# The fifth group's first dense product without a seven-block set, and the order of the pieces around two batches of attention steps

## The chip, the core and the metric

The kernel runs on one core of a Trainium2 chip. Its time is the device time of one execution in microseconds (us); the figure of a kernel is the median of its runs. The profile's own clock, the span, goes from the first to the last instruction and is a little shorter than the time of the same execution.

## The reference

A decayed linear attention with blocks of 64 positions feeds a two-layer network with a tanh GELU. Cut to what is computed:

```python
batch, n_heads, seq, head_dim = (4, 8, 768, 64)       # q, k, v
for b in range(nb):                                    # blocks of 64
    intra = np.einsum('bhic,bhjc->bhij', qb, kb) * Dmask[None]
    intra = np.einsum('bhij,bhjd->bhid', intra, vb)
    inter = np.einsum('bhid,bhde->bhie', qb * lam_pow[None], kv_state)
    out[:, :, sl] = intra + inter
    kb_dec = kb * rev_pow[None]
    kv_state = lam_block[None, :, None, None] * kv_state + np.einsum('bhsd,bhse->bhde', kb_dec, vb)
...
x = np.ascontiguousarray(attn_out.transpose(0, 2, 1, 3)).reshape(B * S, H * D)   # 3072 x 512
h = x @ w_in                                           # 512 x 2048
g = 0.5 * h * (1.0 + np.tanh(c * (h + 0.044715 * h * h * h)))
return (g @ w_out).astype(np.float32)                  # 2048 x 512
```

## The kernel before

The attention runs in 24 steps, each of 256 positions of one sequence and half of the heads. For a step n, `load_step` brings q, k and v from memory (queue SP), `prep_qk` scales q on DVE and casts k on ACT into one half-precision tile and sends that tile through a transposing DMA (queue SP, steps from 9 on) into `qkT_n`, and `prep_v` scales v on GpSimd (POOL) and then issues the loads of step n + 3. `scores` multiplies (PE, tiles S), `causal` masks the scores on DVE into `PT_n`, and the state is updated with `update`: a DVE addition into t and a POOL product into u. The output of a step goes through ACT into `xT`, the input of the dense part.

Late steps come in batches. `burst(ns, ss)` issues the scores of the steps ns, the attention output (L424, L449) of the earlier steps ss and the state products (L438, tiles K) of ns, then the masks, then the ACT copies into xT, then the first state update of ns.

The dense part works on seven groups of rows: `groups = [[0, 1], [2], [3], [4, 5], [6, 7], [8, 9], [10, 11]]`, each entry 256 positions of a sequence. The group with number 4, the fifth, covers the steps 12 to 15 and has 512 rows. Its work is cut into pieces, kept in the list `filler`, which `fill(n)` takes from the front, n at a time, wherever the hand-written order of the main part (L904 to L1088) says so. So the order on TensorE is written out: pieces of dense work between the attention's steps.

A plain piece of a 512-row group's first product is `mm1([f])`: four matmuls of 128 x 512 into one PSUM bank (Hps), and one ACT gelu from that bank into `gT`. Sixteen such pieces make the product, in the order f = 0, 8, 1, 9, and so on. The two last groups, 5 and 6, use seven block products in place of eight (`seven(m, k)`): the matrices are halved both ways, sums of input blocks (`sum_x`, DVE) and of weight blocks (`sum_win`, DVE) are formed ahead, and each of seven products m = 1 to 7 is four matmuls of 128 x 256 into the banks HX, HW and HY. Copies (ACT, DVE) and additions (DVE) combine them; the products 1, 6, 7 and 4 follow each other in one bank HX, and what is copied or added out of it between two of them reads that bank. One set k covers four values of f, thus the work of four plain pieces.

Before the change, group 4 (`MIXED`) does one of its four sets, k = 0, in this way: ten pieces, seven of them block products and three plain ones set between, then nine plain pieces. The second product of the group (`product`, tiles MX, MW, MY, also in seven-block form) follows; it needs sums of rows of gT (`sum_g`, DVE, tiles gs), which `behind(k, ...)` hangs behind the k-th piece of the group. The sums of the first half of gT hang behind piece n1 - 7 = 12, counted from 0.

The pools matter here. All PSUM tiles come from eight banks (tag "M"); a new tile waits until the earlier one in its bank was read. `qkT` tiles come from four buffers, PT from three, v16 and qk16 from five, the loaded q32, k32 and v32 from four each. The tiles m1, q and u2 of a seven-block set use buffers of q32 and k32, and the sums xs use one of the three xT buffers.

The main part around the change: group 4 is queued in `R(17, 15)` (L1045). Nine pieces of the group before it are left and are done by the first piece after L1059. Eleven pieces are taken between L1057 and the batch of steps 18 and 19 (L1064), and six between that and the batch of 20 and 21 (L1073).

Of the kernel before, what the change touches and what calls it, by code (L numbers as in the profile page):

```python
# [15 lines left out]
def kernel(  # L16
# [43 lines left out]
    def load_step(s, names="qkv"):  # L60
        b, r = divmod(s, 2 * NSB)
        sb, half = divmod(r, 2)
        ts = ld32.setdefault(s, [])
        for nm, src in (("q", q), ("k", k), ("v", v)):
            if nm not in names:
                continue
            t = ld.tile([P, HH, 2, D], FP32, tag=nm + "32", name=f"{nm}32_{s}")
            rows = src[b, half * HH : (half + 1) * HH, sb * SB : (sb + 1) * SB, :]
            queue = nc.scalar if (nm, s) == ("v", 0) else nc.sync
            pin(queue.dma_start(out=t[:].rearrange("p h j d -> p h (j d)"),  # L70
                                in_=rows.rearrange("h (p j) d -> p h (j d)", j=2)))
            ts.append(t)
# [5 lines left out]
    HF, HE = NF // 2, DM // 2  # L78
# [91 lines left out]
    def load_ahead(s):  # L170
        if s < NSTEP:
            load_step(s)
# [83 lines left out]
    def prep_v(s):  # L256
        scale_v(s)
        if s >= 6:
            if s + 3 == FIRST_DMA_T + 1:
                load_step(s + 3, "qk")  # L260
            else:
                load_ahead(s + 3)

    def scale_v(s):
        tv = a16p.tile([P, 2, HH, D], FP16, tag="v16", name=f"v16_{s}")
        pin(nc.gpsimd.tensor_tensor(wide(tv[:]), ld32[s][2][:], decay(dv, s), ALU.mult))  # L266
        a16[s] = a16[s] + (tv,)

    def prep_qk(s):
        cast_qk(s)  # L270
        transpose_dma(s)

    def cast_qk(s):
        q32, k32, _ = ld32[s]
        tqk = a16p.tile([P, 2, 2, HH, D], FP16, tag="qk16", name=f"qk16_{s}")
        tq, tk = tqk[:, 0], tqk[:, 1]
        q_eng = nc.gpsimd if s == 3 else nc.vector
        pin(q_eng.tensor_tensor(wide(tq), q32[:], decay(dq, s), ALU.mult))  # L278
        if s == 0:
            inverse(halves[0])  # L280
            odd(halves[1])
            inverse(halves[1])
        pin(nc.scalar.activation(out=wide(tk), in_=k32[:], func=AF.Copy))  # L283
        a16[s] = (tq, tk)
        whole_qk[s] = tqk
# [3 lines left out]
    def transpose_dma(s):  # L289
        tqk = whole_qk.pop(s)  # L290
        if s >= FIRST_DMA_T:
            o = qkp.tile([P, 2, 2, 2, P], FP16, tag="qkT", name=f"qkT_{s}")
            pin(nc.sync.dma_start_transpose(out=o[:].rearrange("p a j h t -> p (a j h) t"),
                                            in_=tqk[:].rearrange("p a j h d -> p (a j h d)")))
            qkT[s] = o
            if s == FIRST_DMA_T:
                load_step(s + 1, "v")
# [219 lines left out]
        return gs_kept[1:]  # L517

    SEVEN = (5, 6)
    MIXED = 4  # L520
    sum_xs = []
    SLOTS = {5: {1: 0, 2: 1, 5: 1, 6: 1, 3: 1, 7: 1}, 4: {1: 0, 2: 1, 5: 0, 6: 1, 3: 1, 7: 1}}
    groups = [[0, 1], [2], [3], [4, 5], [6, 7], [8, 9], [10, 11]]
    group_of = {sb: (g, i) for g, sbs in enumerate(groups) for i, sb in enumerate(sbs)}
    filler = []

    def queue_group(g, lead=0, per_set=0):
# [12 lines left out]
        def mm1(fs):  # L540
            Hps = ps_M.tile([P, per, N], FP32, tag="M", name="Hps")
            for i, f in enumerate(fs):
                for c in range(NC):
                    pin(nc.tensor.matmul(by_block(Hps[:, i, :]), w_in16[:, c, f * P : (f + 1) * P],  # L544
                                         x(c), start=(c == 0), stop=(c == NC - 1)))
            f = fs[0]
            dst = gT[:, f, :, :] if per == 2 else gT[:, f % HF, f // HF : f // HF + 1, :]
            pin(nc.scalar.activation(out=dst, in_=Hps[:], func=AF.Gelu_apprx_tanh))  # L548
# [151 lines left out]
        def seven(m, k):  # L700

            st = of_set.setdefault(k, {})
            for name in {1: "X", 2: "W", 5: "Y"}.get(m, ""):
                key = name + str(k % 2) if name == "X" else name
                if key not in hbank:
                    hbank[key] = ps_M.tile([P, 2, SB], FP32, tag="M", name="H" + name)
                st[name] = hbank[key]
            dst = st[{2: "W", 5: "Y", 3: "Y"}.get(m, "X")]
            a, b = X_FACTORS[m]
            for i in range(2):  # L710
                f = 2 * k + i
                for c in range(2):
                    pin(nc.tensor.matmul(  # L713
                        dst[:, i, :],
                        w_in_block(a, slice(c, c + 1), slice(f * P, f * P + P))[:, 0],
                        x_block(b, slice(c, c + 1))[:, 0],
                        start=(m in (1, 2, 5) and c == 0 and i == 0), stop=(m in (2, 3, 4) and c == 1),
                        skip_group_check=True))

            def copied(name, tag, eng):  # L720
                t = ld.tile([P, HH, 2, D], FP32, tag=tag, name=f"{name}_{g}_{k}")
                t = t[:].rearrange("p h j d -> p (h j d)").rearrange("p (i t) -> p i t", i=2)
                if eng is nc.scalar:
                    pin(nc.scalar.activation(out=t, in_=dst[:], func=AF.Copy))
                else:
                    pin(eng.tensor_copy(out=t, in_=dst[:]))
                st[name] = t

            def gelu(F, T, src):
                pin(nc.scalar.activation(out=gT[:, 2 * k : 2 * k + 2, F, T * SB : T * SB + SB],  # L730
                                         in_=src, func=AF.Gelu_apprx_tanh))

            def added(F, T, name):
                pin(nc.vector.tensor_tensor(st[name], dst[:], st[name], ALU.add))
                pending.append(lambda src=st[name]: gelu(F, T, src))

            if m == 1:
                copied("m1", "q32", nc.scalar)
            elif m == 2:
                added(0, 0, "m1")  # L740
            elif m == 5:
                copied("q", "q32", nc.scalar)
                release()
            elif m == 6:
                copied("u2", "k32", nc.vector)
            elif m == 3:
                added(0, 1, "u2")
            elif m == 7:
                added(1, 1, "q")
            elif m == 4:  # L750
                pending.insert(0, lambda: gelu(1, 0, dst[:]))
            if (k == HF // 2 - 1 or g == MIXED) and m in (3, 7, 4):
                release()

        def merge(lead, per_set):
# [71 lines left out]
        def behind(k, i0, i1, ms):  # L827

            piece = filler[at + k]

            def both():
                piece()
                sum_g(i0, i1, ms)

            filler[at + k] = both
# [3 lines left out]
        if g in SEVEN:  # L839
# [6 lines left out]
            for k, m in enumerate((2, 4, 3)):  # L846
                behind(len(parts) * k, 4, 8, (m,))
            return
        if g == MIXED:
            sum_xs.append(sum_x)  # L850
            plain = [[f] for i in range(2, HF) for f in (i, i + HF)]
            for m in (1, 0, 2, 5, 0, 6, 3, 0, 7, 4):
                filler.append((lambda m=m: seven(m, 0)) if m else (lambda fs=plain.pop(0): mm1(fs)))
            for fs in plain:
                filler.append(lambda fs=fs: mm1(fs))
        for i in range(HF) if g != MIXED else ():
            for fs in ([[i, i + HF]] if per == 2 else [[i], [i + HF]]):
                filler.append(lambda fs=fs: mm1(fs))
        for m, p in order:
# [3 lines left out]
        n1 = HF * (2 // per)  # L863
        if per == 2:
            behind(5, 0, 4, (1, 2))
            behind(6, 0, 4, (4, 3))
            behind(7, 4, 8, (1,))
            behind(8, 4, 8, (2,))
            behind(9, 4, 8, (4,))
            behind(10, 4, 8, (3,))  # L870
        else:
            n1 += 3 * (g == MIXED)
            behind(n1 - 7, 0, 4, (1, 2) if g == 3 else (1, 2, 4, 3))
            if g == 3:
                behind(12, 0, 4, (4, 3))
            w = 2 if g + 1 in SEVEN else 1
            for k, m in zip((0, 3, 7, 11) if w == 2 else (0, 1, 2, 4), (1, 2, 4, 3)):
                behind(n1 + k, 4, 8, (m,))

    def fill(n):  # L880
        for _ in range(min(n, len(filler))):
            filler.pop(0)()
# [17 lines left out]
    def U(n):  # L900
        update(n, 1)
# [152 lines left out]
    sum_win(4, 0, nc.vector)  # L1054
    fill(2)
    sum_win(4, 1, nc.vector)
    for m in (1, 2, 3, 4):  # L1057
        sum_xs[0](m)
    prep_qk(20)  # L1059
    fill(3)  # L1060
    prep_qk(21)
    fill(8)

    burst((18, 19), (16, 17))  # L1064
    prep_v(20)
    fill(2)
    U(18)
    U(19)
    prep_v(21)
    fill(2)  # L1070
    prep_qk(22)
    fill(2)
    burst((20, 21), (18, 19), 11, 4)  # L1073
# [43 lines left out]
```

## Time and profile before

| | us |
|---|---|
| runs | 203.12, 202.26, 202.57 |
| median | 202.57 |
| the profiled execution, its time | 203.12 |
| its span | 201.3 |

The chain of work that ended last takes 81% of the span on PE, 6% in DMA, 5% on DVE and 4% in the SP queue. The granted TensorE clock is 0.998. The work that the change touches lies between 113 and 132 us. All of the span before 113 us is issued by lines that the change leaves as they are.

A row of the timeline has the start in us, the duration, the engine, the line and operation, the output and input tiles with their shapes, and in brackets how long the engine had been idle before it and what ended that. A row of the chain has start, duration and the work that stood on the chain there. In a table by stretches each engine has its busy time and number of instructions; the granted clock, the DMA engines' share and GB/s come last. Matmuls are pipelined, so that the duration of one in the timeline is longer than its distance to the next one.

### The profile page before, as it was taken

How to read it: one execution, taken by the hardware profiler on the slowest of the kernel's cores; microseconds unless marked ns; L12 is line 12 of the kernel's file. 1: busy time of each engine (PE TensorE's matmuls, PEld its weight loads, DVE VectorE, ACT ScalarE, POOL GpSimd, SP SyncE). 2: the span in 40 equal slices, each digit the busy share in tenths (PEclk: the TensorE clock that was granted, in tenths of full speed). 3: DMA queues.
4: the chain of work that ended last, by engine and by line, in shares of the span. 5: the costliest groups of instructions: out<-in, count | busy, mean ns of one | idle time of the engine just before them, and what ended most of it. 6: DMA issues, size and time to landing. Idle time of an engine off the chain costs nothing.

```text
span 201.3 us, 5970 instructions
## 1 busy us (share of the span) xinstructions
PE 192.3 (96%) x2451; PEld 141.5 (70%) x2451; DVE 159.8 (79%) x304; ACT 123.8 (61%) x253; POOL 74.7 (37%) x85
## 2 busy tenths in 40 slices
PE   8979999999999999998999989799999999999993
PEld 2546544456888888653689855468888888888882
DVE  4888623689999989969989969999778997588720
ACT  2663878375883774677535676563668845778321
POOL 6594123457458633638334204729002030002000
PEclk9999999999999999999999999999999999999999
DMA  5999999999999999997985944940112200020205
GB/s 165 292 327 385 387 384 382 290 288 314 333 249 214 265 260 212 263 249 144 284 192 129 247 150 85 266 72 0 31 24 104 103 10 0 0 107 0 107 0 208
DMA packets 61722, 37.86 MB, mean 188 GB/s; under 512 B 17536, under 2 KB 54656, under 8 KB 61696
## 3 DMA queue, kind: packets, MB, share of 16 engines
q1 hardware_dynamic: 61152, 37.23, 73.2%
q8 instruction: 19, 0.31, 0.7%
q10 hardware_dynamic: 544, 0.26, 0.5%
q14 instruction: 7, 0.06, 0.1%
HBM read 27.26 MB, written 6.29 MB: 167 GB/s over the span
## 4 chain that ended last, share of the span: by engine, by line
PE 81%; DMA 6%; DVE 5%; SPq 4%; issue 1%; ACT 1%
PE Hps L544 18%; PE MX L621 17%; PE MY L621 9%; PE HX L713 8%; PE O2ps L559 7%; PE MW L621 4%; PE HY L713 4%; SPq L70 4%; DMA wi<-in_moe_w_in_dram 4%; PE Hps L804 3%; PE S L340 3%; DMA qkT<-qk 3%; PE HW L713 2%; DVE gs L591 2%; DVE PT L350 2%; PE OK L398 2%
## 5 line engine op out<-in xcount | busy, mean ns | idle before, releaser
L501 POOL TENSOR_TENSOR u<-t,lumask 128x256 f16<-128x256 f32 x40 | 30.6, 780 | 51.3 <-DVE t L494 28.0
L544 PE MATMUL Hps<-xT,w_in 128*128 128x512 f16 (+1 forms) x272 | 47.7, 329 | 0.5 <-DVE PT L350 0.5
L544 PEld LDWEIGHTS <-w_in 128*128 128x128 f16 x272 | 26.2, 98 | 17.4 <-issue 0.6
L548 ACT ACTIVATE gT<-Hps 128x512 f16<-128x512 f32 x52 | 30.7, 602 | 8.7 <-PE Hps L544 8.2
L621 PEld LDWEIGHTS <-gs 128*128 128x128 f16 x320 | 31.2, 98 | 3.6
L350 DVE TENSOR_TENSOR PT<-S,mask 128x512 f16<-128x512 f32 x48 | 30.4, 681 | 3.7 <-PE S L340 3.4
L266 POOL TENSOR_TENSOR v<-v,dv 128x512 f16<-128x512 f32 x24 | 29.9, 1249 | 7.5 <-DMA v<-in_v_dram 7.2
L621 PEld LDWEIGHTS <-gT 128*128 128x128 f16 x240 | 23.2, 98 | 3.6 <-ACT gT L548 0.5
L621 PE MATMUL MX<-w_sum,gs 128*128 128x256 f16 x160 | 21.4, 273 | 0.0
L591 DVE TENSOR_TENSOR gs<-gT 128x1024 f16<-128x1024 f16 (+1 forms) x24 | 19.1, 802 | 1.2 <-ACT gT L548 1.2
L278 DVE TENSOR_TENSOR qk<-q,dq 128x512 f16<-128x512 f32 x23 | 19.6, 853 | 0.6 <-DMA q<-in_q_dram 0.5
L283 ACT ACTIVATE qk<-k 128x512 f16<-128x512 f32 x24 | 15.1, 629 | 7.0 <-DMA k<-in_k_dram 7.0
L666 POOL TENSOR_TENSOR o<-u,q 128x512 f32<-128x512 f32 (+1 forms) x5 | 5.4, 1088 | 37.3 <-ACT u L638 37.3
L713 PEld LDWEIGHTS <-ws 128*128 128x128 f16 x144 | 14.0, 97 | 2.4
L559 PE MATMUL O2ps<-w_out,gT 128*128 128x512 f16 x64 | 14.6, 379 | 0.0
L475 ACT ACTIVATE xT<-OK 128x256 f16<-128x256 f32 x26 | 10.1, 462 | 7.3 <-PE OK L398 7.3
L638 ACT ACTIVATE u<-MX 128x256 f32<-128x256 f32 x18 | 6.9, 383 | 10.2 <-PE MX L621 10.2
L475 ACT ACTIVATE xT<-O 128x256 f16<-128x256 f32 x22 | 8.0, 460 | 8.3 <-PE O L449 6.3
L713 PEld LDWEIGHTS <-w_in 128*128 128x128 f16 x108 | 10.5, 98 | 2.6 <-issue 1.0
L340 PE MATMUL S<-qkT 64*64 64x128 f16 x384 | 9.4, 221 | 2.7 <-DMA qkT<-qk 1.9
L340 PEld LDWEIGHTS <-qkT 64*64 64x64 f16 x384 | 6.0, 106 | 8.5 <-issue 3.0
L713 PE MATMUL HX<-xs,ws 128*128 128x256 f16 x72 | 10.8, 273 | 0.0
(95 smaller groups left out, 330.7 us busy)
## 6 DMA issues: line engine op xcount, KB each, us to landing
q<-in_q_dram SPq DMA_DIRECT2D x24, 256.0 KB, 5.0
k<-in_k_dram SPq DMA_DIRECT2D x24, 256.0 KB, 5.3
v<-in_v_dram SPq DMA_DIRECT2D x23, 256.0 KB, 5.4
out_dram<-o SPq DMA_DIRECT2D x19, 256.0 KB, 2.3
wo<-in_moe_w_out_dram SPq DMA_DIRECT2D x4, 1024.0 KB, 9.5
wi<-in_moe_w_in_dram SPq DMA_DIRECT2D x4, 512.0 KB, 6.8
wi<-in_moe_w_in_dram SPq DMA_DIRECT2D x2, 1024.0 KB, 12.4
out_dram<-o SPq DMA_DIRECT2D x2, 512.0 KB, 4.9
```

Source lines behind the costliest of these rows:

```text
L266: pin(nc.gpsimd.tensor_tensor(wide(tv[:]), ld32[s][2][:], decay(dv, s), ALU.mult))
L278: pin(q_eng.tensor_tensor(wide(tq), q32[:], decay(dq, s), ALU.mult))
L340: pin(nc.tensor.matmul(Sps[hl][half64(c), hp, jk, :], o[half64(hl), 1, jk, hp, half64(c)], o[half64(hl), 0, :, hp, half64(c)], start=True, ...
L350: pin(nc.vector.tensor_tensor(t[:, hl].rearrange("p b c d -> p b (c d)"), Sps[:].rearrange("p b c d -> p b (c d)"), mask[:].unsqueeze(1).t ...
L475: pin(nc.scalar.activation(out=d, in_=o, func=AF.Copy))
L501: pin(nc.gpsimd.tensor_tensor(u[:], state[half][:].unsqueeze(2).to_broadcast([P, 2, 2, D]), lumask[:, 2 * half : 2 * half + 2, :].unsqueez ...
L544: pin(nc.tensor.matmul(by_block(Hps[:, i, :]), w_in16[:, c, f * P : (f + 1) * P], x(c), start=(c == 0), stop=(c == NC - 1)))
L548: pin(nc.scalar.activation(out=dst, in_=Hps[:], func=AF.Gelu_apprx_tanh))
L559: pin(nc.tensor.matmul(O2[tau][0][:], gT[:, f % HF, f // HF, tau * P : (tau + 1) * P], w_out16[:, f, :], start=(n == 0), stop=(n == NF - 1)))
L591: pin(nc.vector.tensor_tensor(g_rows(m, i), g_rows(a, i), g_rows(b, i), op))
L621: pin(nc.tensor.matmul(dst, lhsT, rhs, start=(opens and i == 0), stop=(closes and i == HF - 1), skip_group_check=True))
L713: pin(nc.tensor.matmul(dst[:, i, :], w_in_block(a, slice(c, c + 1), slice(f * P, f * P + P))[:, 0], x_block(b, slice(c, c + 1))[:, 0], sta ...
```

## The change

It takes the seven-block set out of group 4. All sixteen pieces of its first product are plain again, in the order 0, 8, 1, 9, and so on; the four `sum_x` of that group go, and so do the two ACT copies, the DVE copy and the three DVE additions of the set. The number of gelu instructions stays at sixteen. The sums of the first half of gT hang behind piece 9, counted from 0; in both kernels ten plain pieces' worth of the group's work is done by then.

In the main part the fill counts are set for that: five pieces instead of ten lie between the end of the previous group's pieces and the batch of 18 and 19, and eight instead of six between that batch and the batch of 20 and 21. `prep_v(20)`, with the loads of step 23, moves ahead of the batch of 18 and 19; `prep_v(21)` moves to where `prep_v(20)` was.

```diff
     SEVEN = (5, 6)
-    MIXED = 4
-    sum_xs = []
...
-            if (k == HF // 2 - 1 or g == MIXED) and m in (3, 7, 4):
+            if k == HF // 2 - 1 and m in (3, 7, 4):
                 release()
...
-        if g == MIXED:
-            sum_xs.append(sum_x)
-            plain = [[f] for i in range(2, HF) for f in (i, i + HF)]
-            for m in (1, 0, 2, 5, 0, 6, 3, 0, 7, 4):
-                filler.append((lambda m=m: seven(m, 0)) if m else (lambda fs=plain.pop(0): mm1(fs)))
-            for fs in plain:
-                filler.append(lambda fs=fs: mm1(fs))
-        for i in range(HF) if g != MIXED else ():
+        for i in range(HF):
             for fs in ([[i, i + HF]] if per == 2 else [[i], [i + HF]]):
                 filler.append(lambda fs=fs: mm1(fs))
...
-            n1 += 3 * (g == MIXED)
-            behind(n1 - 7, 0, 4, (1, 2) if g == 3 else (1, 2, 4, 3))
+            behind(9, 0, 4, (1, 2) if g == 3 else (1, 2, 4, 3))
...
     sum_win(4, 1, nc.vector)
-    for m in (1, 2, 3, 4):
-        sum_xs[0](m)
+    fill(2)
     prep_qk(20)
-    fill(3)
+    fill(1)
     prep_qk(21)
-    fill(8)
+    prep_v(20)
+    fill(3)
 
     burst((18, 19), (16, 17))
-    prep_v(20)
+    prep_v(21)
     fill(2)
     U(18)
     U(19)
-    prep_v(21)
-    fill(2)
+    fill(4)
     prep_qk(22)
     fill(2)
     burst((20, 21), (18, 19), 11, 4)
```

More of the change, by code (lines that the diff above doesn't have):

```diff
@@ L1056 @@
     sum_win(4, 1, nc.vector)
-    for m in (1, 2, 3, 4):
-        sum_xs[0](m)
+    fill(2)
     prep_qk(20)
+    fill(1)
+    prep_qk(21)
+    prep_v(20)
     fill(3)
-    prep_qk(21)
-    fill(8)
     burst((18, 19), (16, 17))
-    prep_v(20)
+    prep_v(21)
     fill(2)
```

## The prediction

> **What bounds the kernel now.** I read the page first, then a table by stretches around the changed place, then the chain of waits and the timeline there. The page:
>
> ```profile
> PE 192.3 (96%) x2451; PEld 141.5 (70%) x2451; DVE 159.8 (79%) x304; ACT 123.8 (61%) x253; POOL 74.7 (37%) x85
> ```
>
> TensorE sets the time; only its products and its few gaps matter. The stretches (span of each, then busy time of PE, PEld, DVE, ACT, POOL):
>
> ```profile
> 113.66:120.45 6.79, 6.01 (x44) 3.91 (x41) 5.26 (x9) 5.46 (x11) 0.43 (x1) 1.00 0.72 192
> 120.45:122.18 1.73, 1.73 (x105) 1.69 (x105) 1.27 (x3) 0.70 (x2) 0.00 (x0) 1.00 0.00 0
> 122.18:127.45 5.27, 5.27 (x27) 2.24 (x24) 5.20 (x12) 4.61 (x10) 3.78 (x5) 1.00 0.78 171
> 127.45:131.00 3.55, 1.99 (x102) 1.64 (x101) 3.55 (x5) 1.52 (x4) 2.34 (x2) 1.00 0.98 253
> 131.00:158.40 27.40, 27.40 (x240) 22.99 (x243) 23.33 (x42) 17.85 (x37) 7.16 (x7) 1.00 0.19 42
> ```
>
> The first is the seven-block set, the second the batch of steps 18/19, then six products, then the batch of 20/21, which takes 3.55 us where the one before took 1.73. From 131.00 on PE has no gap for 27 us, so what is won or lost by 131.00 stays. The chain leaves PE exactly here:
>
> ```profile
> 118.70 0.45 PE HX L713 x4
> 119.16 0.02 issue
> 119.18 0.70 DVE q L734
> 119.88 0.04 issue
> 119.92 0.60 PE HX L713 x4
> 120.52 0.40 PE S L340 x16
> 120.92 2.47 DVE PT L350 x4
> ...
> 128.89 1.45 DVE qk L278
> 130.34 0.61 DVE PT L350
> 130.96 0.04 issue
> 131.00 2.75 PE Hps L544 x12
> ```
>
> The set's last block product waits for DVE to read its PSUM bank; then a DVE chain from 120.92 to 130.95 releases the bank of the first product behind the second batch. A second wait stands beside that chain, in the timeline:
>
> ```profile
> 122.20 2.00 SPq L293 DMA_TRANSPOSE qkT<-qk  x1
> 125.00 1.53 SPq L293 DMA_TRANSPOSE qkT<-qk  x1
> 128.93 0.42 PE L340 MATMUL S<-qkT 64*64 64x128 f16 x16 [1.06 <-DMA qkT<-qk]
> ```
>
> Transpositions of 20 and 21 go out only when the batch of 18/19 has freed their qkT buffers (the pool has four), and 21 lands 3.9 us after its issue, too late.
>
> **The change, part by part.** Up to the 113.77 start of the set the queues hold the same work. I place the changed kernel's instructions on that clock.
>
> *PE work.* Seven block products of 0.44 us and three dense ones of 0.865 (chain rows "HX x4", "Hps x4") are 5.66 us; the set took 6.68 (113.77 to 120.45), so about 1.0 is waiting. It becomes four dense products, 4 x 0.865 = 3.46, instead of 7 x 0.44 = 3.08: +0.4 us of PE work. That the seven-block form really is cheaper is the cost of this change.
>
> *Order.* By the fill counts 13 dense products' worth of work lies ahead of the batch of 20/21 in both; but the batch of 18/19 now stands behind five of them (before: seven), and eight lie between the batches (before: six).
> PE: 113.77 + 5 x 0.87 = 118.12, first batch starts (before 120.45).
> Batch 1.73 (its row above, which has no wait). Its last banks are those of products four and five, so its state products wait for their gelus: A gelu starts 0.27 us behind its product and runs 0.60 (rows "0.27 <-PE Hps", 0.60), and two casts of k (0.62 each) now stand between the gelus: by that the fifth ends near 119.2, and PE arrives at 118.12 + 0.92 = 119.05 (before: 120.45 to 121.37). Bounds 0 and 0.62 (one cast in the way); I take 0.2: 120.05.
> Eight products by 5.27/6 = 0.878: 7.02, 127.07.
> Second batch 1.73, and 0.15 for the same gelu wait behind the cast of k 22: 128.95, against 131.00.
> Gain 2.05 us, if nothing else holds that point. Three things could.
>
> *Transpositions.* Slots free at 120.05 - 0.1. Before, the store of the fifth output tile was queued between them (issue at 124.31); now both stores stand ahead of the first. SP rows of a transposition are 1.24 to 2.54 us, issue to landing 3.1 to 3.9 by the seven issues of this stretch, once 5.04 on the chain (90.59). With 2.0 and 3.9, 21 lands at 119.95 + 2.0 + 3.9 = 125.9; needed at 127.5. Hidden, with 1.6 us to spare.
>
> *The DVE chain.* Removed: four sums of x (2.5 us from 112.55 to 115.04), one copy and three additions of 0.69, 5.3 us in all. It costs PE only the 0.78 wait (already in the 1.0). The chain now starts at 118.12 + 0.46 = 118.58: four masks 2.48, state updates until 118.58 + 3.65 = 122.23 (before: 120.91 to 124.56). New wait: the first sum of gT needs the gelu of product eight, third behind the batch: 120.05 + 3 x 0.878 + 0.27 + 0.60 = 123.55, so DVE idles 1.3. Behind it on DVE stand three sums, the cast of q 22 and the masks of 20/21; PE's product 14 waits for the first mask's bank. Those four sums and the cast took 5.78 before (124.56 to 130.34); alone each takes 0.68 (rows at 152.86 and 143.21), 3.4 together. The excess, 2.38, goes with 5.34 us of POOL work inside it: 0.45 per POOL us. Now one scaling of v (that of 20) is already done, at 114 to 116, and POOL ends near 126.2: u pair 1.18 from 121.4, v of 21 1.49, u pair 2.07. Overlap 2.65 us, excess 1.2: 123.55 + 4.6 + 0.61 = 128.76, just before PE's 128.95. Taken as hidden; bounds 3.4 (127.56) and 5.78 (129.94).
>
> The Trainium skill, page "SBUF — State Buffer", section "Who interferes with whom", says a DVE instruction with two SBUF inputs and a GpSimd one that reads SBUF take a shared port in turn, the second blocked until the first ends. Here the row of a sum beside v's scaling is 1.42 us and not 0.68, but full blocking would make 3.4 + 5.34 = 8.74 of the 5.78 measured, so the trace agrees only in kind. By it the stretch would be 3.4 + 2.65 = 6.05 and product 14 would start at 130.2 (an estimate), 0.8 us won.
>
> *Moved steps.* Scaling of v 20 (1.49 us, POOL) goes ahead of the first u pair; POOL idles 9.6 us there. Its three load issues for step 23 (0.80, 0.53, 0.51 on SP) stay directly behind transposition 21 and go out some 3 us earlier; the data are read at 143. Scaling of 21 passes the second u pair, which only the batch of 22/23 reads. Casts of k 20/21 move between gelus (in the 0.2). Output store of the group: earlier by 10 us, waited for by nobody here. All nothing; without POOL's idle time the u pair would be 1.49 late, still 4 us early for its reader. Fewer buffers turn in the rings of xT and of q and k; the next users are loads and sums that have landed long since.
>
> **Sum.** +0.4 of work, -1.0 waiting in the set, -1.8 in the second batch, +0.35 of new waits: -2.05. Profiled span 201.3 to 199.25; that execution's time was 203.12, the slowest of three, median 202.57: 202.57 - 2.05 = **200.5 us**.
>
> **Rivals.**
> (a) *The DVE chain decides.* Contention as strong as before: first mask done at 123.55 + 5.78 + 0.61 = 129.94, product 14 at 129.98, gain 1.0: 201.5. For: DVE works without a gap from 120.91 to 131 in the old rows. Against: one v scaling less beside it. 0.14. The Trainium skill's page "SBUF — State Buffer" ("Who interferes with whom") would end here too, near 201.8 by the estimate above.
> (b) *Wait moves on.* The 1.8 of the second batch stays (transposition still late, or PE 2 us ahead meets DVE after 131, 23.33 of 27.40 busy); only 1.0 - 0.4 - 0.3 is won: 202.3. Against: eight products where six stood. 0.09.
> (c) *Slower: the two transpositions, now back to back, with the loads of 23 directly behind.* If each holds SP for 2.54 and 21 lands only with those loads: v of 23 issued at 119.95 + 5.08 + 1.41 = 126.44, landing 5.0 later (loads' median), 131.4; scores of 21 to product 14 took 1.57 (128.93 to 130.50): 133.0, 2.0 lost, 204.6. It decides from a landing past 129.4. For: the engines' share was 0.98 while 21 and the loads overlapped. Against: they overlapped then too, and 21 landed 3.9 us after issue. 0.17, which also covers a late partner I can't see.
> That the words of the change also name the batch of 13/14 is no rival: no line ahead of the set moves.
>
> **How the numbers follow.** The forecast 0.60, its own range 199.8 to 201.2 (waits 0 to 1.2, and the 0.3 to 0.5 by which single runs lie off the median). About 0.5%, 1.0 us, is what a measurement can tell. Faster by more: the forecast and 0.10 of (a): 0.70. Within: rest of (a), (b), 0.01 of (c): 0.14. Slower: 0.16. Range 199.7 to 202.4: holds the forecast, (a), (b); leaves out (c).
>
> **What would show it.** Right: batch of 18/19 near 118.1 and of 20/21 near 127.1; no PE gap for the transposition, none ahead of the first batch over 0.2; product 14 near 129 with the first mask ending just before; the rest of the span as long as before (about 70.3 us). Wrong: a gap before the scores of 21, gT sums beginning after 124, the mask of 20 ending past 129.5, or a new gap behind product 14.

## The result, and the profile after

| | median us | runs | ratio to the kernel before (95% interval) |
|---|---|---|---|
| before | 202.32 | 6 (201.91 to 203.12) | |
| after | 199.77 | 6 (199.53 to 200.25) | 0.9874 (0.9850 to 0.9897) |

The changed kernel is 2.55 us faster; 2.05 were forecast. The time forecast was 200.5 us, worked out from the 202.57 of the first three runs of the kernel before; with three more its median is 202.32. The measured 199.77 lies at the lower edge of the range of 199.7 to 202.4. The profiled spans are 201.3 and 197.7 us, 3.6 apart, of which 1.1 lie ahead of the change: in the execution profiled before, which was the slowest of its six, the scores of step 16 waited 0.84 us near 95 us for their transposition, and the one profiled after did not, with the same instructions there. From its first piece on, the changed part can be compared directly. The same table by stretches, cut at the same instructions as before (set or five products, first batch, products between, second batch, then 27.4 us more):

```profile
112.65:117.06 4.41, 4.41 (x23) 1.86 (x20) 1.27 (x1) 3.57 (x7) 2.17 (x2) 1.00 1.16 300
117.06:118.79 1.73, 1.73 (x106) 1.69 (x105) 1.27 (x3) 0.60 (x1) 0.00 (x0) 1.00 0.78 292
118.79:125.79 7.00, 7.00 (x36) 3.03 (x33) 5.89 (x14) 5.81 (x12) 4.22 (x5) 1.00 0.93 160
125.79:127.32 1.53, 1.53 (x101) 1.49 (x101) 1.53 (x3) 1.00 (x2) 0.00 (x0) 1.00 0.58 153
127.32:154.70 27.38, 27.38 (x243) 22.97 (x240) 22.86 (x42) 18.20 (x39) 7.16 (x7) 1.00 0.16 40
```

In every row PE is busy for the whole stretch. From the first piece to the first product behind the second batch it takes 14.67 us (112.65 to 127.32), before 17.23 (113.77 to 131.00): 2.56 us, the whole gain of the medians. Behind it lie 70.4 us, before 70.3. The chain of waits no longer leaves PE there:

```profile
112.81 4.32 PE Hps L542 x20
117.13 0.57 PE S L340 x32
117.70 0.45 PE O L424 x32
118.15 0.25 PE K L438 x32
118.40 0.55 PE O L449 x8
118.95 6.91 PE Hps L542 x32
125.86 0.57 PE S L340 x32
126.43 0.45 PE O L424 x32
126.88 0.28 PE K L438 x32
127.16 0.33 PE O L449 x4
127.49 2.59 PE Hps L542 x12
```

What stood on the chain before now runs beside it. In the timeline:

```profile
118.81 2.66 SPq L293 DMA_TRANSPOSE qkT<-qk  x2
122.21 0.81 DVE L589 TENSOR_TENSOR gs<-gT 128x1024 f16<-128x1024 f16 x1 [1.04 <-ACT gT L546]
125.58 0.68 DVE L278 TENSOR_TENSOR qk<-q,dq 128x512 f16<-128x512 f32 x1
126.25 2.48 DVE L350 TENSOR_TENSOR PT<-S,mask 128x512 f16<-128x512 f32 x4
```

Both transpositions go out together. The sums of gT wait 1.04 us for the eighth product's gelu, as forecast, and are done early all the same: the first of the four masks (126.25, 0.69 us by itself) ends at 126.94, and PE needs its bank at 127.32, 0.38 us later.

### The profile page after: what moved, and what is told of

The parts are those of the page before. It is cut to its first block, busy times and chain, and to the rows that moved or that the text cites. A ratio compares the mean times of both kernels' runs of the same rounds, so it can differ in the third digit from the quotient of the medians.

```text
span 197.7 us, 5935 instructions
## 1 busy us (share of the span) xinstructions
PE 191.4 (97%) x2439; PEld 139.8 (71%) x2439; DVE 154.0 (78%) x296; ACT 122.8 (62%) x251; POOL 75.1 (38%) x85
## 4 chain that ended last, share of the span: by engine, by line
PE 88%; SPq 4%; DMA 4%; ACT 1%; issue 1%
PE Hps L542 24%; PE MX L619 17%; PE MY L619 9%; PE HX L711 7%; PE O2ps L557 7%; PE MW L619 4%; DMA wi<-in_moe_w_in_dram 4%; SPq L70 4%; PE HY L711 4%; PE S L340 3%; PE Hps L802 3%; PE HW L711 2%; PE OK L398 2%; PE O L449 1%; PE O L424 1%; PE Tps L311 1%
## 5 line engine op out<-in xcount | busy, mean ns | idle before, releaser
L542 PE MATMUL Hps<-xT,w_in 128*128 128x512 f16 (+1 forms) x288 | 50.8, 332 | 0.0
L542 PEld LDWEIGHTS <-w_in 128*128 128x128 f16 x288 | 27.8, 98 | 19.1
L546 ACT ACTIVATE gT<-Hps 128x512 f16<-128x512 f32 x56 | 33.1, 598 | 9.3 <-PE Hps L542 8.8
L619 PEld LDWEIGHTS <-gT 128*128 128x128 f16 x240 | 23.2, 98 | 3.6 <-ACT gT L546 0.5
L589 DVE TENSOR_TENSOR gs<-gT 128x1024 f16<-128x1024 f16 (+1 forms) x24 | 17.6, 737 | 1.5 <-ACT gT L546 1.5
L711 PEld LDWEIGHTS <-ws 128*128 128x128 f16 x128 | 12.5, 97 | 1.8
L557 PEld LDWEIGHTS <-gT 128*128 128x128 f16 x64 | 6.1, 98 | 6.6
L619 PE MATMUL MY<-w_out,gs 128*128 128x256 f16 x80 | 10.7, 273 | 0.0
L589 DVE TENSOR_TENSOR gs<-gs,gT 128x1024 f16<-128x1024 f16 (+1 forms) x12 | 10.2, 852 | 0.3
```

Source lines behind the costliest of these rows:

```text
L557: pin(nc.tensor.matmul(O2[tau][0][:], gT[:, f % HF, f // HF, tau * P : (tau + 1) * P], w_out16[:, f, :], start=(n == 0), stop=(n == NF - 1)))
L589: pin(nc.vector.tensor_tensor(g_rows(m, i), g_rows(a, i), g_rows(b, i), op))
L619: pin(nc.tensor.matmul(dst, lhsT, rhs, start=(opens and i == 0), stop=(closes and i == HF - 1), skip_group_check=True))
L711: pin(nc.tensor.matmul(dst[:, i, :], w_in_block(a, slice(c, c + 1), slice(f * P, f * P + P))[:, 0], x_block(b, slice(c, c + 1))[:, 0], sta ...
```

## The experiments

"Stretch" is the time from the start of the group's first piece to the start of the first product behind the second batch, in the profile of each run. The runs were taken in three groups, each with the kernel before beside it: it had 202.09 us beside e1 to e4, 202.13 beside e5 to e8 and 202.16 beside e9 to e11, and the ratios are to these.

| run | median us | ratio (95%) | stretch us |
|---|---|---|---|
| before | 202.32 | | 17.23 |
| after | 199.77 | 0.9874 (0.9850 to 0.9897) | 14.67 |
| e1 plain, seven and six | 200.80 | 0.9935 (0.9911 to 0.9958) | 15.84 |
| e2 after, v 20 behind | 200.02 | 0.9900 (0.9871 to 0.9929) | 15.11 |
| e3 before, five qkT | 203.26 | 1.0063 (1.0030 to 1.0096) | 17.22 |
| e4 before, plain product between | 201.41 | 0.9965 (0.9944 to 0.9985) | 16.59 |
| e5 set kept, reordered | 202.74 | 1.0024 (1.0006 to 1.0042) | 17.13, two products more |
| e6 before, v 20 ahead | 201.42 | 0.9949 (0.9924 to 0.9975) | 16.57 |
| e7 as e6, transposition 20 later | 201.29 | 0.9952 (0.9934 to 0.9970) | 16.51 |
| e8 after again | 199.82 | 0.9878 (0.9847 to 0.9908) | 14.67 |
| e9 after, ten between | 201.93 | 0.9987 (0.9971 to 1.0003) | 16.40, two products more |
| e10 after, six and seven | 200.22 | 0.9889 (0.9864 to 0.9914) | 14.99 |
| e11 after, four and nine | 199.66 | 0.9874 (0.9845 to 0.9904) | 14.67 |

### e1: the old positions with plain products

```diff
     prep_v(20)
-    fill(3)
+    fill(5)
...
     U(19)
-    fill(4)
+    fill(2)
```

> The changed kernel with the old positions: seven plain products ahead of the batch of 18/19 and six between the batches. If the gain comes from the set and its DVE work being gone and from the stores no longer standing between the two transpositions (the first theory), the second batch finds its transposition landed and the DVE chain, started 1.8 us later, ends some 0.3 us behind TensorE: 0.3 us slower than the changed kernel (0 to 0.7), and still some 2.2 us faster than the kernel before. If the positions alone carry the gain (the rival), the old 1.8 us wait of the second batch comes back: 1.8 us slower than the changed kernel.

It is 1.17 us longer in the stretch than the changed kernel, more than the 0 to 0.7 expected and less than the rival's 1.8. The chain of waits and, below it, a row of PE's timeline:

```profile
118.94 0.40 PE S L340 x16
119.34 2.47 DVE PT L350 x4
...
127.92 0.61 DVE PT L350
128.53 0.04 issue
128.57 2.75 PE Hps L542 x12
```

```profile
128.57 2.75 PE L542 MATMUL Hps<-xT,w_in 128*128 128x512 f16 x12 [1.00 <-DVE PT L350]
```

No wait for a transposition is left, so that was hidden as the first theory said, though closely: 21 landed at 125.88, when the second batch was just beginning (125.87) with the scores of 20. But PE waits 1.00 us for DVE: the chain from the first mask of 18 to the first mask of 20 took 9.2 us (119.33 to 128.53), and with six products between the batches PE is through with the second batch before that. I had taken the chain too short, because its sums, which no longer wait for a gelu here, meet all of GpSimd's work: 4.95 us for sums and cast, in the changed kernel 4.04. So, with the set gone, the positions are worth 1.17 us, by the time that they give DVE.

### e2: the scaling of v 20 behind the first batch

```diff
-    prep_v(20)
     fill(3)
     burst((18, 19), (16, 17))
-    prep_v(21)
+    prep_v(20)
...
     U(19)
+    prep_v(21)
     fill(4)
```

> The changed kernel with the scaling of v 20 and the loads of step 23 back behind the batch of 18/19, as in the kernel before. If GpSimd's work beside DVE's sums sets the length of the DVE chain at 0.45 us per us (the first theory), the sums and the cast lengthen by some 0.7 us from the 4.05 of the changed kernel, the first mask ends 0.2 us behind TensorE's arrival: 0.2 us slower (0 to 0.6). If GpSimd's scaling does not matter, the same time; if the shared port blocks in full, 1.5 us more on the chain and 1.0 us slower.

0.25 us slower by the medians (200.02 against 199.77), 0.44 in the stretch. In the timeline, the scaling of v 21, a sum of gT beside it, and the wait at the end:

```profile
124.35 1.48 POOL L266 TENSOR_TENSOR v<-v,dv 128x512 f16<-128x512 f32 x1
124.86 1.52 DVE L589 TENSOR_TENSOR gs<-gT 128x1024 f16<-128x1024 f16 x1
127.64 2.75 PE L542 MATMUL Hps<-xT,w_in 128*128 128x512 f16 x12 [0.27 <-DVE PT L350]
```

The sum takes 1.52 us here and 0.68 in the changed kernel, where GpSimd is one scaling further by then. It ends at 126.38, 0.55 us after the scaling does (125.83). Sums and cast take 4.82 us against 4.04. The 1.5 us that the expectation gave to full blocking are not what it would cost: the scaling's 1.48 us hold a wait of its own, as is shown below under the DVE chain.

### e3: transposition 20 early, in the kernel before

```diff
-    qkp = ctx.enter_context(tc.tile_pool(name="qkp", bufs=4))
+    qkp = ctx.enter_context(tc.tile_pool(name="qkp", bufs=5))
-    ubp = ctx.enter_context(tc.tile_pool(name="ubp", bufs=4))
+    ubp = ctx.enter_context(tc.tile_pool(name="ubp", bufs=3))
```

> The kernel before with five buffers of qkT in place of four (room from the u tiles, three in place of four): transposition 20 goes out before the batch of 18/19, and 21 directly when that batch frees its buffer, so that it lands before the second batch. If the DVE chain holds the first product behind the second batch (the first theory), it starts where it did, from 10.0 to 10.5 us after the first batch's start: the stretch from the set to that product shortens by 0 to 0.4 us. If the late transposition is what holds it (the rival), the stretch shortens by 1.1 to 1.5 us.

The stretch is as long as before, 17.22. PE's timeline:

```profile
126.93 0.64 PE L340 MATMUL S<-qkT 64*64 64x128 f16 x32
129.32 0.32 PE L438 MATMUL K<-v,qk 64*64 64x64 f16 x16 [1.18 <-POOL v L266]
130.47 2.75 PE L544 MATMUL Hps<-xT,w_in 128*128 128x512 f16 x12 [0.50 <-DVE PT L350]
```

All scores run at once, so the wait for the transposition is gone; its 1.06 us came back as 1.18 for the scaled v 21, and behind it the DVE chain decides as before. The wait that the profile named was not the one to remove. The whole kernel became 1.2 us slower somewhere else, about 0.8 of it behind the stretch (130.47 to 201.6); why, was not tried.

### e4: a plain product between the seventh and the fourth block product, in the kernel before

```diff
-            for m in (1, 0, 2, 5, 0, 6, 3, 0, 7, 4):
+            for m in (1, 0, 2, 5, 6, 0, 3, 7, 0, 4):
```

> The kernel before with the three plain products at other places among the seven block products, one of them between the seventh and the fourth, so that the fourth does not wait for DVE's addition out of its bank. If that wait is a cost by itself (the first theory), the first batch starts 0.7 us earlier, the DVE chain with it, and the time falls by 0.7 us (0.5 to 1.0). If the wait is only passed on to the second batch (the rival: the chain there is bound by something that does not move), the time stays within 0.2 us.

0.68 us faster, 0.64 in the stretch. The first batch starts 6.04 us after the start of the set (before: 6.68), and the second batch keeps both its waits, 1.01 for the transposition and 0.43 for DVE: the set's own wait was a cost by itself. Seven plain products take 6.14 us in e1, so in this order the set is the cheaper of the two, by 0.1 us.

### e6 and e7: the kernel before, relieved at the second batch

e6 moves the scaling alone; e7 also sends transposition 20 behind the last output store of the group (the lines marked e7).

```diff
-    prep_qk(20)                        # e7
+    cast_qk(20)                        # e7
     fill(3)
+    transpose_dma(20)                  # e7
     prep_qk(21)
+    scale_v(20)
     fill(8)
     burst((18, 19), (16, 17))
-    prep_v(20)
+    load_step(23)
+    scale_v(21)
...
     U(19)
-    prep_v(21)
     fill(2)
```

> The kernel before with the scaling of v 20 alone moved ahead of the batch of 18/19 (the loads of step 23 stay behind it). Two limits stand side by side at the second batch, the DVE chain and the late transposition 21. The chain's sums and cast should take 4.95 us in place of 5.78, as in e1, which is 0.8 us; but with transposition 21 as late as before TensorE itself reaches the first product behind the batch only 0.5 us earlier: 0.5 us faster than the kernel before (0.3 to 0.6). If the transposition binds nothing (the rival), 0.8 us.

> As e6, with transposition 20 queued behind the group's last output store, so that 20 and 21 follow each other directly. The wait for transposition 21 goes (e1 had none with this order), and only the DVE chain is left: 0.8 us faster than the kernel before (0.7 to 1.0), thus 0.3 us more than e6. If the order of the queue does not matter, the same as e6.

e6 gained 0.71 us, 0.66 in the stretch, a little over the 0.3 to 0.6 expected; e7 gained 0.84 and 0.72. Of e6 and then of e7, the waits in PE's timeline:

```profile
127.92 0.42 PE L340 MATMUL S<-qkT 64*64 64x128 f16 x16 [1.04 <-DMA qkT<-qk]
129.23 2.75 PE L544 MATMUL Hps<-xT,w_in 128*128 128x512 f16 x12
```

```profile
126.45 0.64 PE L340 MATMUL S<-qkT 64*64 64x128 f16 x32
129.15 2.75 PE L544 MATMUL Hps<-xT,w_in 128*128 128x512 f16 x12 [1.00 <-DVE PT L350]
```

In e6 the transposition holds PE and the DVE wait is gone; in e7 it is the other way round, and the product starts at nearly the same place. The two limits lay within 0.1 us of each other, closer than the 0.3 that was expected.

### e5: the set kept, with eight products between the batches

On top of e7 it has e4's order of the set, and

```diff
     U(19)
-    fill(2)
+    fill(4)
```

> The seven-block set kept, with the plain products placed as in e4, v of 20 scaled ahead of the batch of 18/19, transposition 20 behind the group's last output store, and eight plain products instead of six between the batches. If the set's loss lay in its two waits and in the positions alone (the first theory), what is left is its cheaper TensorE work: 0.4 us faster than the changed kernel (0.2 to 0.6), 0.985 of the kernel before. If DVE's additional 5 us of work for the set come back as waits elsewhere (the rival), no faster than the changed kernel, 0.987 or more.

A clear miss: 2.9 us slower than the changed kernel. Its positions are not those of the changed kernel either: the set and its three plain products are seven products' worth ahead of the first batch, where the changed kernel has five, so the eight between leave one behind the second batch in place of three. Three waits in PE's timeline:

```profile
117.29 0.60 PE L713 MATMUL HX<-xs,ws 128*128 128x256 f16 x4 [0.53 <-DVE u L726]
140.31 0.60 PE L713 MATMUL HX<-xs,ws 128*128 128x256 f16 x4 [1.07 <-DVE u L726]
184.68 0.60 PE L713 MATMUL HX<-xs,w_in 128*128 128x256 f16 x4 [0.82 <-DVE q L734]
```

The first is the set again: the scaling of v 20 now runs beside the sums of x, one of which takes 1.26 us (at 113.24) in place of 0.41, and DVE's copy out of HX comes late. The two others are in the groups behind, which e9 tells apart from the set. No run keeps the set and leaves three products behind the second batch with eight between, so what a set placed like that would cost is not shown.

### e9, e10 and e11: how many products where

All three change only fill counts of the changed kernel: ahead of the first batch, between, and behind the second, in place of five, eight, three: five, ten, one (e9); six, seven, three (e10); four, nine, three (e11).

> The changed kernel with ten plain products between the batches and one behind the second, in place of eight and three. If the products behind the second batch are DVE's cover for the sums that the next group's block products wait for (the theory formed on e5), the two products that are gone there come back as waits of the block products near 140 us, and the shifted pieces as waits near 180: 1 to 3 us slower than the changed kernel. If the loss of e5 is the set's own DVE work (the rival), the same time within 0.3 us.

> The changed kernel with six plain products ahead of the batch of 18/19 and seven between the batches, halfway to e1. The DVE chain from the first batch's masks to the first mask of 20 took 9.2 us in e1 and 9.35 with a wait of 1.04 in the changed kernel; TensorE reaches the first product behind the second batch 1.73 + 7 x 0.877 + 1.53 = 9.40 us after the first batch's start, the chain ends 0.46 + 9.2 = 9.66 after it: a wait of 0.3 us, 0.3 us slower than the changed kernel (0.1 to 0.5), a quarter of e1's loss. If each product of position is worth the same (the rival), 0.6 us.

> The changed kernel with four plain products ahead of the batch of 18/19 and nine between the batches. The chain is hidden with 0.45 us to spare at five and eight, so one more product of lead has nothing to hide: the same time as the changed kernel within 0.2 us. If positions go on paying (the rival), 0.3 to 0.6 us faster.

e9 is 2.1 us slower than the changed kernel (201.93 against 199.82), with no seven-block set in the group at all. Its PE timeline:

```profile
128.97 1.03 PE L542 MATMUL Hps<-xT,w_in 128*128 128x512 f16 x4
139.57 0.60 PE L711 MATMUL HX<-xs,ws 128*128 128x256 f16 x4 [1.06 <-DVE u L724]
183.94 0.60 PE L711 MATMUL HX<-xs,w_in 128*128 128x256 f16 x4 [0.82 <-DVE q L732]
```

From the first product behind the second batch to the end it takes 70.9 us with two products (1.75 us) fewer to do; the changed kernel takes 70.4 with them. The changed kernel has no wait of PE behind the second batch. Those products were the cover for DVE's states, sums of x and sums of gT, and the shifted pieces of the later groups also wait, near 184, where the chain leaves PE for DVE's sums and copies. So the two later waits of e5 (1.07 and 0.82) come from its positions, not from its set.

e10 lost 0.32 us in the stretch where 0.3 were expected, and its product waits 0.15 us for DVE's mask. e11 has the stretch of the changed kernel to 0.01 us and the same time.

e8, the changed kernel again, agreed with its first measurement:

> The changed kernel again, on the chip of the three before, to compare them with: 0.987 of the kernel before (0.985 to 0.990).

## Why the prediction was right

*The set.* Forecast: 0.4 us more of TensorE work against 1.0 of waiting, 0.6 won. From e7 to e1 the set goes and little else: 16.51 to 15.84, 0.67. Of this 0.13 is a wait that e7's set has and the set before has not (6.81 us against 6.68), so against the kernel before it is 0.54 (6.68 to 6.14). The five products took 4.41 us where 4.35 were forecast. e4 shows the waiting part by itself, 0.64, without removing the set: the set's loss was its wait, and a better order inside the set wins as much as taking it out.

*The second batch.* Forecast: 1.8 us of waits gone. Two parts did it, each measured: GpSimd's scaling and the order of the transpositions, 0.72 (before to e7; 0.85 from the first batch on, less the 0.13 in the set), and the positions, 1.17 (e1 to after); 1.89 together. Taking away one wait meets the next: e3 gained nothing, and e6 0.66 with the transposition's wait left.

*The transposition.* Forecast landed 1.6 us ahead of its need. In the changed kernel 21 landed at 124.4, 1.4 us before the second batch starts with the scores of 20. The two sizes behind that were both off and cancel in part: the second transposition went out 1.4 us after the first and not 2.0, and 21 landed 4.2 us after its issue and not 3.9. No run with both transpositions behind the store waited for one (after, e1, e2, e7). Rival (c), slower by a late landing beside the loads of 23, is excluded by them; rival (b) too, by 27.38 of 27.38 us of PE behind the batch.

*The DVE chain.* Forecast first batch plus 10.6 us for the end of the first mask, 0.2 ahead of PE; measured 9.9 (117.06 to 126.94), 0.38 ahead. Mis-sized was the contention, 4.6 us for sums and cast and measured 4.04; the sums also began 0.28 us earlier than forecast. Rival (a) had 5.78 us there; with the scaling of v 20 ahead of the batch even e1 took only 4.95.

The prediction also had the kind of contention wrong. It took DVE to be slowed by 0.45 us per us of GpSimd work. The rows of the kernel before, DVE's and GpSimd's in one order of time, show turns:

```profile
124.24 0.61 POOL L501 TENSOR_TENSOR u<-t,lumask 128x256 f16<-128x256 f32 x1
124.47 0.93 DVE L591 TENSOR_TENSOR gs<-gT 128x1024 f16<-128x1024 f16 x1
124.81 1.49 POOL L266 TENSOR_TENSOR v<-v,dv 128x512 f16<-128x512 f32 x1
125.44 1.42 DVE L591 TENSOR_TENSOR gs<-gs,gT 128x1024 f16<-128x1024 f16 x1
126.27 2.07 POOL L501 TENSOR_TENSOR u<-t,lumask 128x256 f16<-128x256 f32 x2
126.89 0.99 DVE L591 TENSOR_TENSOR gs<-gT,gs 128x1024 f16<-128x1024 f16 x1
127.80 1.10 DVE L591 TENSOR_TENSOR gs<-gT 128x1024 f16<-128x1024 f16 x1
128.31 1.49 POOL L266 TENSOR_TENSOR v<-v,dv 128x512 f16<-128x512 f32 x1
128.81 1.53 DVE L278 TENSOR_TENSOR qk<-q,dq 128x512 f16<-128x512 f32 x1
```

Add start and duration: the sums and the cast each end 0.55 us after the end of the GpSimd instruction that was running when they started (124.85 to 125.40, 126.30 to 126.86, 128.34 to 128.90, 129.80 to 130.34; the first of the two u products of one row ends at 127.33, the third sum at 127.88), and a scaling of v ends 0.90 us after the sum that was running when it started (125.40 to 126.30, 128.90 to 129.80).

Beside an idle DVE the scaling takes 1.04 us (the changed kernel's, at 121.42), so 0.45 of its 1.49 us is its own wait. The prediction added GpSimd's 5.34 us, waits included, to DVE's 3.4, and so found 8.74 us for full blocking, far above the 5.78 measured; that sum counts the waits twice, and its 6.05 us for the changed kernel does too. Counted by turns, the changed kernel has the rest of a scaling (0.26 us), three sums behind GpSimd (0.55 each), two u products between them (0.47 each) and a sum and a cast that meet nothing (0.60 each): 4.05 us for the 4.04 measured. That the chain is hidden was forecast rightly, but by a rate that only averages such turns, and with 4.6 us it was 0.2 us from not being so: there is some luck in it.

The Trainium skill's page "SBUF — State Buffer", section "Who interferes with whom", has the second of the two engines blocked until the first ends. The trace agrees, in the rows above and in e2, where the sum ended 0.55 us after the scaling beside it.

*The term that was off.* "+0.35 of new waits", for gelus ahead of the state products, found nothing: the fifth gelu ran from 117.17 to 117.77, before PE came to its bank at 117.98. And the second batch needs less than the first, 1.53 us for the 1.73 that I gave it, because steps 18 and 19 begin a sequence and half of their positions have no earlier state to multiply (4 matmuls of L449 for 8, 0.23 us for 0.46). 0.35 + 0.2 is about what the gain of 2.56 has over 2.05. Another 0.25 us between the forecast time and the measured one is only the lower median of the kernel before.

*What the prediction did not see.* I took the seventh and eighth product between the batches as free. In the change they come from ahead of the first batch, and there they are free. e9 shows that this does not hold for the products behind the second batch: two more, taken from there, cost 2.1 us.

## What to carry to other kernels

When a profile names one wait, work out where the waiting engine would stand without it: here a late transposition, a late scaling and a chain on another engine held the same product to within about half a microsecond of each other, and taking the transposition's wait away alone gained nothing. When two engines lengthen each other's instructions, follow the ends of their rows before taking a mean rate: a duration that holds a wait must not be added to the other engine's. A cheaper form of a product that gives additional work to a busy engine can cost more than it saves, and whether it does depends on its order (e4); count that engine's chain to its next reader, not its mean busy share. Independent work between two dependent bursts is cover with a budget, and moving it is worth no more than the other engine's lag (e11 gained nothing beyond that), and less once the place that it was taken from starts to wait.

## What the runs showed of the hardware

Beside GpSimd a sum of two half-precision tiles on DVE took 0.8 to 1.5 us, alone 0.68. The two engines took turns: in the kernel before, the changed kernel and e2, a DVE sum or cast that met a GpSimd product ended 0.55 us after it, and a GpSimd product that met a sum ended after it by 0.47 us (u, 0.61 us beside no sum) or 0.90 us (v, 1.04 us beside an idle DVE). Two transposing DMAs of 256 KB in a row held the SP queue for 2.66 us in the changed kernel and 3.39 in e1, the first of the two alone 2.00 before; the second landed 3.9 to 4.2 us after its issue in these three.
